# Eight visits of 128 tokens and one of 256 in the first list of a convolution and expert kernel, in place of ten of 128

## The chip, the core and the metric

The kernel runs on one core of one Trainium2 chip. A core has five engines that work side by side, each through its own queue in order: TensorE (PE, matmuls and transposes), VectorE (DVE), ScalarE (ACT), GpSimd (POOL) and SyncE (SP), which here only issues transfers. Sixteen DMA engines move data between the large memory (HBM) and the on-chip memory (SBUF). Results of matmuls lie in PSUM. The metric is the device time of one execution in microseconds.

## The reference, cut to what matters

```
w   = softmax(weight_gen) over 7 taps            # per token and head
x1  = sum over k of w[..., k] * x[token - 6 + k] # 8 heads of 24 columns, 8 x 2880 tokens
g   = argmax(x1 @ w_group)                       # 4 groups
e   = argmax(x1 @ w_expert[g])                   # 4 experts in each: 16 in all
out = p_g * p_e * (relu(x1 @ w1[g, e]) @ w2[g, e])   # 192 -> 1024 -> 192
```

All is fp32: 23,040 tokens of 192 columns, and every token goes through one of 16 experts, whose weights are 768 KB for each of the two matrices.

## The kernel before

**Groups.** The convolution runs over 15 groups of 12 tokens for each of the 128 partitions (1,536 tokens each), counted from 0. For a group SP loads the taps (`wt`, line 124) and the tokens (`xin`, line 134) into one of two buffers each; VectorE does the softmax and then 2 chunks of products (`pr`, line 317). The sums of the first chunks run on TensorE (line 358), later ones on VectorE (line 335). Then comes the routing: TensorE transposes and scores (lines 418 to 436), ScalarE copies between (lines 411 to 439), VectorE ranks, ScalarE's exponentials (line 375) and TensorE's counting matmuls (lines 476, 477) between, and GpSimd scatters the rows into `rows` in HBM, sorted by expert (line 531).

**Lists and visits.** After some groups `table` makes lists on VectorE (lines 553 to 621): which expert to visit, and from which row. ROUNDS says after how many groups, and how many visits of 384, 256 and 128 tokens. A visit loads one expert's weights and a block of its rows (`xb`, line 822). A visit of 128 in these rounds is plain: fp32 weights (`wa`, line 839, and `wc`, line 852), transposes at line 921. A visit of 256 loads the weights into `raw` (lines 841, 848) and splits them into a high and a low part (ScalarE lines 865 and 874, VectorE line 889); ScalarE copies part of the rows (`xd`, line 914), TensorE transposes them at line 932, and VectorE takes the low part of those too. Both then do the first matmul (line 958), a relu (line 967), the second matmul (line 1004), a scaling (line 1031) and a store of outputs (line 1042). A list of 128s is worked through in order of the experts. In the first list V1 to V10 are the visits of 128; the second list has four visits of 256, V11 to V14.

**What sets the order.** The program writes each engine's order down beforehand. `blocks` goes from unit to unit (a quarter of a visit here) and puts in what the next visits need; between the units `fill` takes steps of `front`, which yields the convolution and routing operation by operation, until a modelled VectorE clock has caught up. Loads of a visit are asked for three visits ahead (plain) or more. Two rules concern the change. In `front` (lines 716 and 717) the next group is loaded at one step of a group's convolution:

```
if n == (2 if state["slots"] else 0) and 1 <= g < ENDS[-1] - 1:
    load_group(g + 1)
```

and in `blocks` (lines 1128 to 1131) `slots` becomes true when the first visit that is not plain is opened:

```
if not b.plain:
    while state["open"]:
        assert step() is not False
    state["slots"] = True
```

SP issues its transfers in program order, and one that waits holds up all behind it.

Of the kernel before, what the change touches and what calls it, by code (L numbers as in the profile page):

```python
# [17 lines left out]
DRAM = bass.MemoryType.DRAM  # L18

WIDTHS = (12,) * 15  # L20
ROUNDS = ((2, 0, 0, 10), (3, 0, 4, 0), (4, 0, 5, 0), (5, 0, 7, 0), (6, 0, 5, 0), (7, 0, 7, 0), (8, 0, 5, 0), (9, 0, 6, 0), (10, 0, 7, 0), (11, 0, 5, 0), (12, 1, 4, 0), (13, 0, 5, 0), (14, 0, 6, 0), (15, 3, 2, 2))
SHORT = (7, 4)
LATE = (1.0, 3.0, 3.0)
AHEAD = (1.0, 1.0, 2.5)
# [18 lines left out]
def conv_moe_kernel(ctx: ExitStack, tc: tile.TileContext, x, wgen, w_group, w_expert, w1, w2, out):  # L43
# [26 lines left out]
    MAXB = NTOK // BK  # L70
    NR = len(ROUNDS)
    ENDS = [r[0] for r in ROUNDS]
    COL = [sum(WIDTHS[:g]) for g in range(len(WIDTHS) + 1)]
# [3 lines left out]
    TB = 3  # L77

    FIRST = ENDS[0]
    MAIN = next(r[0] for r in ROUNDS if r[1] or r[2])  # L80
    kinds = ((3, 1), (2, 2), (1, 3))
    CUT = {4: 3, 5: 2}
    rows_of = {1: UB, 2: 2 * UB, 3: 3 * UB, 4: 2 * UB + HB, 5: UB + HB}
# [2 lines left out]
    sure = 0  # L86
    for r in ROUNDS[:-1]:
        for nb, c in kinds:
            sure = max(sure, min(sure + nb * UB * r[c], COL[r[0]] * P - NE * (nb * UB - 1)))
    left = (NTOK - sure + NE * (BK - 1)) // BK  # L90
    TAIL = max(0, -(-(left - ROUNDS[-1][2]) // TB))

# [452 lines left out]
    def table(r):  # L545
# [14 lines left out]
        if last:  # L560
# [6 lines left out]
            for nb, odd, start, slots in ((4, half, at, SHORT[0]), (5, two, None, SHORT[1])):  # L567
# [4 lines left out]
                yield 0.6  # L572
        todo = [(nb, c) for nb, c in ((kinds[0], kinds[2], kinds[1]) if last else kinds) if ROUNDS[r][c] or last and nb == 2]
        for nb, c in todo:
# [97 lines left out]
    def front():  # L672
# [7 lines left out]
        def pace(g):  # L680
            return 99 if g <= FIRST else HURRY if g < MAIN + 3 else 8 if g in ENDS else 2

# [102 lines left out]

    order = []
    for r, spec in enumerate(ROUNDS):
        for nb, c in kinds:
            order += [(r, nb, q) for q in range(spec[c])]
            if r == NR - 1:  # L790
                order += [(r, k, q) for j, k in enumerate(CUT) if CUT[k] == nb for q in range(SHORT[j])]
# [479 lines left out]
```

## Time and profile before

| | |
|---|---|
| median of 3 runs | 1163.09 us (1161.98 to 1166.91) |
| the profiled execution | 1161.11 us, of which span 1159.1 us |
| TensorE busy | 1104.1 us (95%) |
| VectorE busy | 950.8 us (82%) |
| ScalarE busy | 648.5 us (56%) |
| GpSimd busy | 583.6 us (50%) |
| moved by DMA | 275.06 MB, mean 237 GB/s |

The span runs from the first to the last instruction. Busy shares are averages over stages with different limits, so the rows further down are taken by stage: the stage of the first list lies between 115 and 200 us. Durations of matmuls are pipelined; times between starts are the safer ones. PEclk is the granted TensorE clock, 1.00 for 2.4 GHz and 0.50 for 1.2 GHz. SPq stands for SP's issuing of transfers; their landing comes later.

### The profile page before, as it was taken

To read this page: it belongs to the slowest core of one execution; us is meant where nothing else is said; L and a number is where in the kernel's file an instruction comes from. 1 tells how busy PE (TensorE), PEld (TensorE's weight loads), DVE (VectorE), ACT (ScalarE), POOL (GpSimd) and SP (SyncE) were. 2 spreads that over 40 slices of the span, in tenths; PEclk is the share of its full clock that TensorE was granted. 3 is DMA by queue.
4 is the path that set the end of the run, shared out by engine and by line. 5 is a ranking of instruction groups with operands and counts; after the bars stand their busy time and mean duration, and the time that the engine had idled before them with its cause. 6 is when DMAs were issued, how large, how long until landed. Compare 5 with 4: busy or idle time off the path is not lost.

```text
span 1159.1 us, 23947 instructions
## 1 busy us (share of the span) xinstructions
PE 1104.1 (95%) x7941; PEld 1034.3 (89%) x7941; DVE 950.8 (82%) x1682; ACT 648.5 (56%) x1307; POOL 583.6 (50%) x613
## 2 busy tenths in 40 slices
PE   5786999999999999999999999999999999999997
PEld 2443888989999999999999999999999999999997
DVE  7899996989999998989898989998764676665661
ACT  1341344656556565665665656555646676667672
POOL 7064085738257573748374748475657321222211
PEclk9998998999999999999999999999999999999999
DMA  5698899986978787878797787876769886666562
GB/s 177 203 316 230 276 301 305 268 276 209 307 211 265 238 295 236 282 230 283 219 300 232 266 259 222 289 226 186 220 195 290 245 247 167 179 196 199 165 221 61
DMA packets 84342, 275.06 MB, mean 237 GB/s; under 512 B 15296, under 2 KB 34160, under 8 KB 82416
## 3 DMA queue, kind: packets, MB, share of 16 engines
q1 hardware_dynamic: 64056, 229.77, 64.1%
q0 software_dynamic: 20032, 43.39, 12.4%
q8 instruction: 64, 1.05, 0.4%
q14 instruction: 70, 0.57, 0.2%
q10 hardware_dynamic: 120, 0.28, 0.1%
HBM read 225.83 MB, written 47.88 MB: 236 GB/s over the span
## 4 chain that ended last, share of the span: by engine, by line
PE 74%; issue 8%; DVE 7%; DMA 4%; POOL 3%; ACT 2%; POOLq 1%; SPq 1%; DVEq 0%; ACTq 0%
PE ph L958 31%; PE py L1004 26%; PE py L1006 3%; DVE pr L317 3%; PE pl L401 2%; PE py L1007 2%; PE tpx L933 1%; PE tpx L932 1%; POOL out L1042 1%; PE ph L358 1%; DMA xb<-rows 1%; POOL rows L531 1%; DVE pr L353 1%; PE pl L1015 1%; PE tp L418 1%
## 5 line engine op out<-in xcount | busy, mean ns | idle before, releaser
L958 PE MATMUL ph<-xh,wa 128*128 128x256 f32 (+3 forms) x1992 | 453.4, 303 | 0.0
L1042 POOL DMA_INDIRECT out<-y,xb x189 | 214.8, 1136 | 402.7 <-ACT y L1031 168.7
L1004 PE MATMUL py<-wc,hh 128*128 128x192 f32 x2160 | 400.2, 326 | 0.0
L958 PE MATMUL ph<-xl,wa 128*128 128x256 f32 (+3 forms) x1328 | 350.0, 285 | 0.6 <-DVE xl L889 0.6
L1004 PEld LDWEIGHTS py<-wc,hh 128*128 128x128 f32 x2160 | 346.0, 190 | 0.0
L958 PEld LDWEIGHTS ph<-xh,wa 128*128 128x128 f32 x1992 | 335.5, 189 | 9.9 <-issue 8.4
L967 ACT ACTIVATE hh<-ph 128x512 f32<-128x512 f32 (+2 forms) x296 | 165.6, 559 | 258.5 <-PE ph L958 256.6
L317 DVE TENSOR_TENSOR pr<-xin,wt 128x1152 f32<-128x1152 f32 x186 | 249.3, 1351 | 5.6 <-PE py L358 3.5
L958 PEld LDWEIGHTS ph<-xl,wa 128*128 128x128 f32 x1328 | 250.8, 189 | 1.0 <-DVE xl L889 0.9
L531 POOL DMA_INDIRECT rows<-xrow,ix x156 | 223.5, 1433 | 46.9 <-POOL ix L530 35.6
L335 DVE TENSOR_TENSOR xrow<-xrow,pr 128x1152 f32<-128x1152 f32 x144 | 194.8, 1353 | 0.7
L889 DVE SCALAR_TENSOR_TENSOR pr<-ph,hh 128x256 fp32r<-128x256 f32 (+2 forms) x128 | 65.8, 514 | 79.7 <-ACT hh L972 42.3
L889 DVE TENSOR_TENSOR wa<-raw,wa 128x1024 fp32r<-128x1024 f32 x83 | 101.3, 1220 | 20.5 <-ACT wa L865 14.8
L530 POOL COPY ix<-posi 128x1 int32<-128x1 int32 x156 | 76.2, 500 | 61.7 <-DMA rows<-xrow,ix 31.9
L1006 PE MATMUL py<-wc,hh 128*128 128x384 f32 x320 | 101.2, 361 | 0.0
L972 ACT ACTIVATE hh<-ph 128x256 fp32r<-128x256 f32 (+2 forms) x128 | 59.0, 461 | 52.5 <-PE ph L958 52.5
L865 ACT CAST wa<-raw 128x1024 fp32r<-128x1024 f32 x83 | 87.2, 1050 | 0.0
L874 ACT CAST wa<-raw 128x1024 fp32r<-128x1024 f32 x83 | 86.4, 1041 | 0.0
L1007 PE MATMUL py<-wc,pr 128*128 128x192 f32 x320 | 80.1, 250 | 0.0
L1031 ACT ACTIVATE y<-py,xb 128x192 f32<-128x192 f32 x175 | 66.1, 425 | 22.0 <-PE py L1004 20.3
L889 DVE TENSOR_TENSOR xl<-tpx,xh 128x512 fp32r<-128x512 f32 (+1 forms) x83 | 56.5, 681 | 14.6 <-ACT xh L938 14.4
L1007 PEld LDWEIGHTS py<-wc,pr 128*128 128x128 f32 x320 | 60.9, 190 | 0.0
(205 smaller groups left out, 1325.6 us busy)
## 6 DMA issues: line engine op xcount, KB each, us to landing
wc<-in_moe_w SPq DMA_DIRECT2D x73, 768.0 KB
raw<-in_moe_w SPq DMA_DIRECT2D x83, 512.0 KB
xin<-in_x SPq DMA_DIRECT2D x14, 1728.0 KB
raw<-in_moe_w SPq DMA_DIRECT2D x91, 256.0 KB
raw<-w1lo SPq DMA_DIRECT2D x83, 256.0 KB
xb<-rows SPq DMA_DIRECT2D x75, 194.0 KB
wa<-in_moe_w SPq DMA_DIRECT2D x24, 384.0 KB
raw<-in_moe_w SPq DMA_DIRECT2D x11, 768.0 KB
```

The source lines that it names most:

```text
L317: nc.vector.tensor_tensor(out=dst, in0=o.xin[:, c0 + k:c0 + k + SC, :].rearrange("p s (h g) -> p s h g", g=HG), in1=w4[:, c0:c0 + SC, :, k ...
L335: nc.vector.tensor_tensor(out=acc, in0=acc, in1=prs[k - 2], op=ALU.add)
L531: written_once(nc.gpsimd.indirect_dma_start(out=rows[:, :], out_offset=bass.IndirectOffsetOnAxis(ap=ix, axis=0), in_=src, in_offset=None, ...
L865: nc.scalar.copy(out=o.wa[:, 0, :], in_=o.raw[0])
L874: nc.scalar.copy(out=o.wa[:, 2, :], in_=o.raw[1])
L889: f(*a, **k)
L958: nc.tensor.matmul(ph[:, v, :], lhsT=w[:, f0:f0 + P], rhs=rhs, start=i == 0, stop=i == len(terms) - 1)
L967: nc.scalar.activation(out=hh, in_=ph, func=AF.Relu)
L1004: nc.tensor.matmul(b.acc[t], lhsT=hh[:, v, c], rhs=wc[0][:, f, :], start=f == 0 and not (b.wide and t == 1), stop=f == NFT - 1 and not (b. ...
L1006: nc.tensor.matmul(b.py[t], lhsT=hh[:, v, c], rhs=wc[f // 4][:, f % 4].rearrange("p l d -> p (l d)"), start=f == 0, stop=False)
L1007: nc.tensor.matmul(b.acc[t], lhsT=hl[:, v, c], rhs=wc[f // 4][:, f % 4, 0, :], start=False, stop=f == NFT - 1)
L1042: ins = nc.gpsimd.indirect_dma_start(out=out[:, :], out_offset=bass.IndirectOffsetOnAxis(ap=b.x.bitcast(I32)[part, t, D + 1:D + 2], axis=0 ...
```

## The change

The first round's entry in ROUNDS becomes one visit of 256 and eight of 128; in the first round the 128s come first; MAIN keeps its value, 3. `table` makes the lists of a round from the larger visits to the smaller, so the first round now has two lists.

```
-ROUNDS = ((2, 0, 0, 10), (3, 0, 4, 0), ...
+ROUNDS = ((2, 0, 1, 8), (3, 0, 4, 0), ...
...
-    MAIN = next(r[0] for r in ROUNDS if r[1] or r[2])
+    MAIN = ENDS[1]
...
-        for nb, c in kinds:
+        for nb, c in kinds if r else kinds[::-1]:
             order += [(r, nb, q) for q in range(spec[c])]
```

V1 to V8 are now the visits of 128, V9 the visit of 256, and V10 is the first visit of the second list.

**SP, after the loads of V8 and V9.** Before: V9's last two rows stand first, then the taps and tokens of the sixth group (g = 5), then V11's raw weights.

```order
L852 ISA
L852 DMA wc_1650<-in_moe_w2 128x1536
L124 DMA wt_1662<-in_weight_gen 128x672
L134 DMA xin_1664<-in_x 128x3456
L836 TENSOR_LOAD tab2_1374
L836 ISA x2
L841 ISA
L841 DMA raw00_193<-in_moe_w1 128x1024
L848 ISA
L848 DMA raw10_195<-in_moe_w1 64x1024
L848 ISA
L848 DMA raw10_195<-w1lo_90 64x1024
```

Now, from the sixth group's taps and tokens on; ahead of them stands the first half of V11's raw weights, and the last row is V10's rows:

```order
L124 DMA wt_1722<-in_weight_gen 128x672
L134 DMA xin_1724<-in_x 128x3456
L848 ISA
L848 DMA raw10_195<-in_moe_w1 64x1024
L848 ISA
L848 DMA raw10_195<-w1lo_90 64x1024
L124 DMA wt_1794<-in_weight_gen 128x672
L134 DMA xin_1796<-in_x 128x3456
L820 TENSOR_LOAD tab2_1394
L820 ISA x2
L822 ISA
L822 DMA xb_175<-rows_89 128x388
```

The sixth group's loads stand there twice, within one visit's raw weights and ahead of V10's rows; the second pair waits for the transfers of the first. The convolution reads only the second pair. All other groups are loaded once.

**VectorE, at the first list** (`units` and `done` count an expert's tokens that are left and taken). Before, from the second operation of the table:

```order
L554 TENSOR_TENSOR units_794<-units_794,origin0_169 128x16
L558 SCALAR_TENSOR_TENSOR units_794<-units_794,done_163 128x16
L607 SCALAR_TENSOR_TENSOR cume_800<-smask12_158,units_794 128x16
L608 TENSOR_TENSOR cums_801<-cume_800,units_794 128x16
L609 TENSOR_SCALAR past_165<-cume_800,qp_151 128x16
```

Now, the first of 18 operations that stand between the second and the third of these:

```order
L558 SCALAR_TENSOR_TENSOR units_794<-units_794,done_163 128x16
L579 TENSOR_SCALAR n2_795<-units_794 128x16
L580 TENSOR_SCALAR n2_795<-n2_795 128x16
L607 SCALAR_TENSOR_TENSOR cume_802<-smask12_158,n2_795 128x16
L608 TENSOR_TENSOR cums_803<-cume_802,n2_795 128x16
L609 TENSOR_SCALAR past_165<-cume_802,qp_151 128x16
```

They make the list of the one visit of 256 and take its tokens off before the list of the 128s.

**ScalarE, around the routing of the third group** (`xT` and `ls` are the third group's transposed tokens and scores, `hh` the relus). Before, the copies of the routing follow one another:

```order
L424 COPY xT_1424<-tp_1673 128x384
L424 COPY xT_1424<-pl_1678 128x384
L431 COPY xT_1424<-pl_1683 128x384
L439 COPY ls_1697<-pl_1693 128x240
L967 ACTIVATE hh_1706<-ph0_1701 128x2x128
```

Now:

```order
L411 COPY rem_1726<-xrow_1027 128x384
L967 ACTIVATE hh_1737<-ph1_1732 128x2x128
L914 COPY xd1_180<-xb_175 128x256
L865 CAST wa_1742<-raw01_194 128x1024
L424 COPY xT_1470<-pl_1744 128x384
L424 COPY xT_1470<-tp_1749 128x384
L424 COPY xT_1470<-pl_1754 128x384
```

V9's copy of rows (line 914) and V10's cast (line 865) moved in front of the routing's copies.

## Rows read from the trace of the kernel before

**Rows 1.** The page's busy times: TensorE's share of the span.

```profile
PE 1104.1 (95%) x7941; PEld 1034.3 (89%) x7941; DVE 950.8 (82%) x1682; ACT 648.5 (56%) x1307; POOL 583.6 (50%) x613
```

**Rows 2.** Busy by stretch: us, PE, PEld, DVE, ACT, POOL, PEclk, DMA share, GB/s.

```profile
180.00:200.00 20.00, 17.31 (x113) 16.91 (x112) 12.37 (x39) 8.71 (x17) 9.53 (x11) 0.83 1.03 295
340.00:380.00 40.00, 40.00 (x305) 38.62 (x305) 36.37 (x43) 25.44 (x49) 30.44 (x26) 1.00 0.84 265
```

**Rows 3.** Timeline of TensorE: start, us, engine, line, operation, idle before and releaser.

```profile
110.78 0.91 PE L358 MATMUL tpx<-pr,ident 128*128 128x384 f32 x2 [1.73 <-DVE pr L353]
...
131.85 0.38 PE L921 MATMUL tp<-ident,xb 128*96 128x128 f32 x2
...
138.25 0.38 PE L921 MATMUL tp<-ident,xb 128*96 128x128 f32 x2
...
187.02 0.66 PE L921 MATMUL tp<-ident,xb 128*96 128x128 f32 x2 [2.69 <-DMA xb<-rows]
...
240.50 0.27 PE L932 MATMUL tpx<-ident,xb 128*128 128x128 f32 x1
...
329.13 0.27 PE L932 MATMUL tpx<-ident,xb 128*128 128x128 f32 x1
...
339.49 0.27 PE L932 MATMUL tpx<-ident,xb 128*128 128x128 f32 x1
```

**Rows 4.** Timeline of SP's issues in the first list's stage.

```profile
156.71 0.87 SPq L839 DMA_DIRECT2D wa<-in_moe_w  x2
...
176.74 0.35 SPq L822 DMA_DIRECT2D xb<-rows  x1
...
225.31 0.34 SPq L822 DMA_DIRECT2D xb<-rows  x1
```

**Rows 5.** Timeline of VectorE: the second round's list of 256s.

```profile
144.78 0.17 DVE L579 TENSOR_SCALAR n<-units 128x16 f32<-128x16 f32 x1
...
147.40 1.35 DVE L317 TENSOR_TENSOR pr<-xin,wt 128x1152 f32<-128x1152 f32 x1
```

**Rows 6.** DMA issues from 110 to 260 us: what, count, KB of one.

```profile
wc<-in_moe_w SPq DMA_DIRECT2D x16, 768.0 KB
wa<-in_moe_w SPq DMA_DIRECT2D x16, 384.0 KB
xin<-in_x SPq DMA_DIRECT2D x3, 1728.0 KB
raw<-in_moe_w SPq DMA_DIRECT2D x9, 512.0 KB
raw<-in_moe_w SPq DMA_DIRECT2D x9, 256.0 KB
xb<-rows SPq DMA_DIRECT2D x8, 194.0 KB
wt<-in_weight_gen SPq DMA_DIRECT2D x3, 336.0 KB
```

**Rows 7.** SP's DMA queue: packets, MB and share; 157 to 187, then 120 to 140 us.

```profile
q1 hardware_dynamic: 2100, 8.06, 83.5%
...
q1 hardware_dynamic: 1543, 6.12, 88.8%
```

**Rows 8.** Timeline of ScalarE at the first visit of 256.

```profile
195.42 0.40 ACT L914 COPY xd<-xb 128x256 f32<-128x256 f32 x1
195.72 1.05 ACT L865 CAST wa<-raw 128x1024 fp32r<-128x1024 f32 x1
```

**Rows 9.** Timeline of GpSimd: first and last scatter of two groups.

```profile
187.91 0.98 POOL L531 DMA_INDIRECT rows<-xrow,ix  x1 [0.33 <-POOL ix L530]
...
221.93 1.80 POOL L531 DMA_INDIRECT rows<-xrow,ix  x1 [0.28 <-DMA raw<-in_moe_w]
...
256.36 0.98 POOL L531 DMA_INDIRECT rows<-xrow,ix  x1 [0.16 <-POOL ix L530]
...
282.90 1.80 POOL L531 DMA_INDIRECT rows<-xrow,ix  x1 [0.28 <-POOL ix L530]
```

More of the change, by code (lines that the diff above doesn't have):

```diff
@@ L20 @@
 WIDTHS = (12,) * 15
-ROUNDS = ((2, 0, 0, 10), (3, 0, 4, 0), (4, 0, 5, 0), (5, 0, 7, 0), (6, 0, 5, 0), (7, 0, 7, 0), (8, 0, 5, 0), (9, 0, 6, 0), (10, 0, 7, 0), (11, 0, 5, 0), (12, 1, 4, 0), (13, 0, 5, 0), (14, 0, 6, 0), (15, 3, 2, 2))
+ROUNDS = ((2, 0, 1, 8), (3, 0, 4, 0), (4, 0, 5, 0), (5, 0, 7, 0), (6, 0, 5, 0), (7, 0, 7, 0), (8, 0, 5, 0), (9, 0, 6, 0), (10, 0, 7, 0), (11, 0, 5, 0), (12, 1, 4, 0), (13, 0, 5, 0), (14, 0, 6, 0), (15, 3, 2, 2))
 SHORT = (7, 4)
```

## Prediction

> **What bounds the kernel now.** I read the page first, then the busy times by stage, then TensorE's own timeline, and last the DMA answers, because TensorE turned out to stand still where a transfer was late. The page gives TensorE 95% of the span [rows 1]. By stages that splits in two: from 340 us on it is busy 40.00 of 40 us at full clock, so nothing there takes a delay back; between 180 and 200 us it is busy 17.31 of 20 and the granted clock is 0.83, which is time at 1.2 instead of 2.4 GHz [rows 2]. What is lost by then is lost at the end too. The timeline names the loss: the transposes of the tenth visit (V10; V1 to V10 are the visits of the first list before) start at 187.02 after 2.69 us of waiting for its rows, xb [rows 3]. SP issued that load at 176.74 [rows 4], so it lay some 10 us in the queue behind what had been issued ahead of it, the next group's x among them. That stretch is bound by the DMA queue, all else by TensorE, and ahead of 111 us by VectorE: the last products of the early convolution keep TensorE waiting 1.73 us at 110.78 [rows 3].
>
> **What the change does, part by part.** The reference's inputs put 167 to 262 tokens on each expert in the first two groups, and one expert has 256 or more. So V9, the new visit of 256, takes the two 128s that the same expert had before, and the other eight experts keep their visits: the coverage is equal, and later lists ask for the same rows. V10 is now the first visit of the second list.
>
> *Less work on TensorE.* Two plain visits of 6.40 us each (131.85 to 138.25) go, one of 10.36 us (329.13 to 339.49) comes [rows 3]: 12.80 - 10.36 = 2.4 us less. The split that V9 needs (two casts on ScalarE, two subtractions on VectorE) lies in front of it, beside plain visits.
>
> *A second list on VectorE.* In front of the list of 128s stands now the list of 256s, 18 small operations. The same list of the second round takes from 144.78 to 147.40 with 17 of them [rows 5]; one more makes 2.8 us. VectorE works without a pause up to the wait at 110.78, so this delays TensorE in full: +2.8. At least it is nothing (if the scatter of rows, which runs beside it, were what ends last), at most 2.8.
>
> *A group loaded twice.* This is what decides. The rule in `front` loads the next group at step 0 of a convolution while `slots` is false and at step 2 when it is true. `slots` turns true when the first visit that isn't plain is opened. That moves from V11 to V9, into the first steps of group 4, so both conditions hold once each: SP's order has wt and xin of the sixth group twice. The second pair goes to the same buffer and waits until the first has landed, with V10's rows right behind it on SP. In bytes [rows 6], from the loads of V8 on: before, V8 and V9 (768 + 97 + 768 each; xb of 128 tokens is half of the 194), wt + xin 2,064, raw of V11 1,024 (512 and twice 256, the second 256 out of w1lo), wa of V10 768, xb 97 = 7,219 KB ahead of and with V10's rows. Now: raw of V9 1,024, V8 1,633, raw of V10 1,024, xb and wc of V9 962, half of raw of V11 512, wt + xin 2,064, the other half 512, wt + xin again 2,064, xb 194 = 9,989 KB, that is 10.23 MB.
>
> When does that land? SP's first load of V8 is issued at 156.71 before [rows 4], now 2.8 later, and the queue is then never empty. SP's queue (q1) moved 8.06 MB in 157 to 187 us, 269 GB/s, and at its best 6.12 MB in 120 to 140 us, 306 GB/s [rows 7]. At 269: 10.23 / 0.269 = 38.0 us, landing at 159.5 + 38.0 = 197.5. At 306: 33.4 us, 192.9. The same sum for before gives 156.7 + 7.39 / 0.269 = 184.2, where TensorE got its rows at 187.0 [rows 3]: it is 2.8 early, since what is issued behind a load shares the engines with its last part. So the late end is 200.3. I take 197.5, from the row of the same stretch, between the two: early by that skew, late because the scatter of rows beside the queue is over in the last third.
>
> When is TensorE there? Before it was ready for V10's transposes at 187.02 - 2.69 = 184.33. Now: + 2.8 from the list; + 1.6 because ScalarE's copy of V9's rows and a 1.05 us cast (the two in [rows 8]) stand ahead of the copies that the third group's routing waits for, and V9's rows land only at 159.5 + 3,875 KB (3.97 MB) / 0.269 = 174.3; + 0.3 for what stands in front of this point in excess (two units of V9 in place of plain ones, less the routing sums that moved behind; the whole visit's saving above holds both). Ready at 189.1, so the wait is 197.5 - 189.1 = 8.4 us in place of 2.7, between 3.8 at the better rate and 11.2 at the late end.
>
> *The clock.* In 180 to 200 us it averages 0.83: 0.17 x 20 = 3.4 us lost, some 0.3 of it while TensorE stood still, so 3.1 [rows 2]. It fell after a wait of 2.7 us; a longer wait gives the same or a little less, since more of the slow time falls into the wait. I leave it at 3.1 (bounds 1.5 to 4).
>
> *The sum*: +2.8 (list) - 2.4 (work) + 1.6 (ScalarE) + 8.4 - 2.7 (the stall, new for old) + 3.1 - 3.1 (its clock) = +7.7. With the stall at 3.8 or 11.2, the clock between its bounds and the list at nothing it runs from -1 to +11. The profiled execution took 1161.1 us, so it would take 1168.8; it lies 2.0 under the median of the runs, 1163.1, so **1171 us** is forecast (1163.1 + 7.7, rounded).
>
> *What the page on DMA makes of it.* The rows show 295 GB/s of all queues in 180 to 200 us at a DMA share of 1.03 [rows 2], and SP's queue alone at 269 [rows 7]. The Trainium skill, "DMA: Bandwidth & Descriptors", section "Where 436 GB/s comes from", says that loads from HBM are limited to about 358 GB/s for a core, and under "Measured" that transfers of 1 MB reach 78% of the peak. By 358 the 10.23 MB would be an estimate of 28.6 us and V10's rows would land before TensorE asks; no run here shows that rate for SP's queue over such a stretch. It would make the third rival true.
>
> **Rivals.**
>
> *Late lists.* ScalarE's exponentials for the third group's ranking, and with them VectorE's ranking and list, stand now behind the copy of V10's rows, and TensorE's counting matmuls behind its transposes. They run at about 197.5 + 3.6 of work + 3.1 of slow clock = 204 instead of just ahead of 184, 20.5 later. The scatter that follows started at 187.91 and issued its last row at 221.93; the next group's took only 256.36 to 282.90; the next list's first load was issued at 225.31, 3.4 after the last row [rows 4, 9]. Now: 208.4 + 26.5 + 2.6 (two stores of outputs between) + 3.4 + 2 to land = 243. TensorE wants it at 240.50 + 7.7 = 248.2 [rows 3]. So there are 5 us to spare, and I count nothing. If the scatter takes 34.0 as before it lands at 250.5: 2.3 us of waiting and another 3.1 of clock, 1168.8 + 5.4 + 2.0 = 1176. For it: VectorE is over 90% busy up to 380 us [rows 2] and catches up little. Against it: the queue is emptier by then.
>
> *A small stall.* If the queue drains near 306 GB/s once the scatter beside it ends, the wait is 3.8, and with a milder clock (1.5) the sum is 7.7 - 4.6 - 1.6 = +1.5: 1164.6, no change that can be told.
>
> *No stall, and faster.* The place is the same, V10's rows; it decides at 10.23 MB in 189.1 - 159.5 = 29.6 us, 346 GB/s on SP's queue. Then the old stall goes with its clock and nothing replaces it: +2.8 - 2.4 - 2.7 - 3.1 + 0.8 (half of ScalarE's delay) = -4.6: 1158.5. For it: the queue did 306 once. Against it: both rows of q1, and the skew seen before.
>
> *The visit of 256 is empty.* If no expert had 256 tokens in the first list, V9 would work on padding and 256 tokens would come back as a further visit, +10.4 [rows 3]: 1181. The margin is 6 tokens of 262 and the inputs are fixed, so this is unlikely.
>
> **How the numbers follow.** The forecast has a chance of 0.50 (1167 to 1174), late lists 0.20 (1174 to 1182), the small stall 0.20 (1162 to 1166), no stall 0.07 (1157 to 1160), the empty visit 0.03. A measurement of this kernel can tell about 0.5%, 5.8 us, from no change, so slower means over 1168.9: three quarters of the forecast's share, all of the late lists and the empty visit, 0.61; faster means under 1157.3, which only the best of the no-stall case reaches, 0.05; the same 0.34. The range leaves out the no-stall case below and the ends above: 1160 to 1181.
>
> **What would show it.** In the profile after: a second xin of 1,728 KB within some 25 us of the first, with SP waiting for a DMA ahead of it; V10's first transposes (line 932) after a wait of 4 to 11 us for xb at about 190 to 200 us; a granted clock of 0.5 behind it; the first plain transposes (line 921) some 2.8 us later; eight plain visits of some 6.4 us and the ninth of some 10.4; no new wait of TensorE beyond 260 us. I am wrong if the wait at V10 is under 2 us (the queue is faster than I read it), if TensorE waits at the next lists' first visits (late lists), or if the first ten visits start no later (the list was hidden).

## The result, and the profile after

The changed kernel takes 1180.08 us (median of six runs, 1176.54 to 1182.17) against 1162.13 us for the kernel before on the same chip: a ratio of 1.0148, 95% interval 1.013 to 1.0166, that is 15 to 19 us slower. The profiled execution took 1182.17 us with a span of 1180.4; before it was 1159.1. The forecast of 1171 had the sign and the first stall right, and less than half of the loss. The measured time lies at the upper end of the stated range (1160 to 1181), which the prediction had kept for late lists, a rival with a chance of 0.20.

The page: busy times, which answer to [rows 1], and the loads of the groups' tokens (issues, KB of one, median us to landing).

```profile
PE 1107.4 (94%) x7917; PEld 1035.3 (88%) x7917; DVE 953.6 (81%) x1702; ACT 651.5 (55%) x1305; POOL 572.6 (49%) x613
...
xin<-in_x SPq DMA_DIRECT2D x15, 1728.0 KB, 12.8
```

TensorE is busy 3.3 us longer. The span grew by 21.3, so 18.0 us of it are standing still; and since the work on TensorE went down by 2.4 us (by the prediction's rows), some 5.7 us more of its busy time than before went to the slow clock. Where this is, the busy times by stretch show, with the columns of [rows 2]; the rows after the gap are wider stretches:

```profile
180.00:200.00 20.00, 14.28 (x104) 12.73 (x104) 8.52 (x23) 8.84 (x18) 3.98 (x5) 0.91 0.95 339
...
240.00:260.00 20.00, 16.88 (x115) 15.03 (x115) 14.48 (x25) 10.82 (x21) 4.54 (x5) 0.91 0.84 292
...
300.00:320.00 20.00, 17.57 (x120) 16.52 (x122) 18.68 (x17) 10.86 (x22) 6.77 (x8) 0.91 0.86 267
...
420.00:460.00 40.00, 30.60 (x215) 28.09 (x214) 34.50 (x35) 17.59 (x33) 26.26 (x23) 0.87 0.82 252
...
460.00:840.00 380.00, 380.00 (x2825) 370.25 (x2824) 350.03 (x617) 226.91 (x426) 218.41 (x218) 1.00 0.78 245
```

The forecast knew of one hole, at 180 to 200 us. There are three more beyond 240 us, the largest around 445 us, each with a granted clock under 1.00. From 460 to 840 us TensorE runs without a pause, so nothing is made good there. TensorE's timeline names the holes (columns and lines as in [rows 3]):

```profile
113.07 0.91 PE L358 MATMUL tpx<-pr,ident 128*128 128x384 f32 x2 [1.73 <-DVE pr L353]
...
134.90 0.38 PE L921 MATMUL tp<-ident,xb 128*96 128x128 f32 x2
...
141.30 0.39 PE L921 MATMUL tp<-ident,xb 128*96 128x128 f32 x2
...
170.38 0.42 PE L921 MATMUL tp<-ident,xb 128*96 128x128 f32 x2 [1.16 <-DMA xb<-rows]
...
179.47 0.44 PE L418 MATMUL pl<-ident,xrow 128*128 128x128 f32 x2 [2.72 <-ACT xT L424]
...
195.81 0.47 PE L932 MATMUL tpx<-ident,xb 128*128 128x128 f32 x1 [4.55 <-DMA xb<-rows]
...
229.63 0.27 PE L932 MATMUL tpx<-ident,xb 128*128 128x128 f32 x1
...
241.69 0.33 PE L932 MATMUL tpx<-ident,xb 128*128 128x128 f32 x1 [1.60 <-DMA xb<-rows]
...
247.88 0.38 PE L418 MATMUL pl<-ident,xrow 128*128 128x128 f32 x2
...
304.21 0.33 PE L932 MATMUL tpx<-ident,xb 128*128 128x128 f32 x1 [2.31 <-DMA xb<-rows]
...
449.82 0.47 PE L932 MATMUL tpx<-ident,xb 128*128 128x128 f32 x1 [9.40 <-DMA xb<-rows]
```

The row at 170.38 is V8, the last visit of 128, which already waits 1.16 us for its rows. The four waits for xb behind it stand at V10, V14, V19 and V31: each is the first visit of a list (the second, third, fourth and sixth). At V10 TensorE waits for the DMA queue, as forecast. At the other three it waits for something else, which SP's own waits show. First SP in 170 to 200 us, in the loads around V10; then SP in 225 to 245, in 285 to 306 and in 420 to 460 us, ahead of V14, V19 and V31; all as queue, line, what was waited for: us in total, times, longest:

```profile
SPq L134 <- DMA xin<-in_x: 5.9, 1, 5.9
SPq L124 <- DMA wt<-in_weight_gen: 5.2, 1, 5.2
...
SPq L822 <- DMA rows<-xrow,ix: 4.3, 1, 4.3
...
SPq L822 <- DMA rows<-xrow,ix: 4.9, 1, 4.9
...
SPq L822 <- DMA rows<-xrow,ix: 12.9, 1, 12.9
```

The first two are the sixth group's second loads of tokens and taps behind the first ones. The others are the loads of rows of V14, V19 and V31, which SP held back until GpSimd's scatter of those rows had landed. Such a wait of SP by itself costs nothing: ahead of the third and the fourth list it was 4.8 and 7.6 us in the kernel before, and TensorE did not wait there. What counts is whether the rows land before TensorE asks. Ahead of the sixth list SP's wait was shorter before (400 to 440 us):

```profile
SPq L822 <- DMA rows<-xrow,ix: 5.6, 1, 5.6
```

So the rows of V31 came late because they were sorted late. GpSimd's timeline, first and last scatter of the third list's group (g = 3, counted from 0; the one at 187.91 and 221.93 in [rows 9]; the prediction and the section on the change call it the third group) and of the sixth list's:

```profile
205.03 0.98 POOL L531 DMA_INDIRECT rows<-xrow,ix  x1 [0.33 <-POOL ix L530]
...
235.89 1.80 POOL L531 DMA_INDIRECT rows<-xrow,ix  x1 [0.28 <-POOL ix L530]
...
413.30 0.98 POOL L531 DMA_INDIRECT rows<-xrow,ix  x1 [0.16 <-POOL ix L530]
...
444.61 0.98 POOL L531 DMA_INDIRECT rows<-xrow,ix  x1 [0.28 <-POOL ix L530]
```

The same for the sixth list in the kernel before:

```profile
395.02 0.98 POOL L531 DMA_INDIRECT rows<-xrow,ix  x1 [0.15 <-POOL ix L530]
...
423.11 1.80 POOL L531 DMA_INDIRECT rows<-xrow,ix  x1 [0.28 <-POOL ix L530]
```

The third list's scatter starts 17.1 us later than before, the sixth's 18.3, and the first visit of the sixth list starts 19.4 later (449.82). In the kernel before it started after a wait of 0.39:

```profile
430.42 0.33 PE L932 MATMUL tpx<-ident,xb 128*128 128x128 f32 x1 [0.39 <-DMA xb<-rows]
```

Why the third list is late stands on VectorE's timeline:

```profile
185.22 0.69 DVE L889 TENSOR_TENSOR xl<-tpx,xh 128x512 fp32r<-128x512 f32 x1 [4.71 <-ACT xh L938]
...
197.32 0.20 DVE L480 TENSOR_REDUCE sme<-exe 128x12 f32<-128x48 f32 x1 [6.36 <-ACT exe L375]
```

and on ScalarE's:

```profile
177.69 0.41 ACT L914 COPY xd<-xb 128x256 f32<-128x256 f32 x1 [1.76 <-DMA xb<-rows]
...
195.79 0.41 ACT L914 COPY xd<-xb 128x256 f32<-128x256 f32 x1 [5.64 <-DMA xb<-rows]
...
197.05 0.24 ACT L375 ACTIVATE exe<-le 128x48 f32<-128x48 f32 x1
```

VectorE, which ranks the group, stands 4.71 us before V9's subtraction, because TensorE has only just transposed V9's rows (ScalarE, which had waited 1.76 us for these rows at 177.69, made the routing's copies late, and with them all that follows on TensorE), and 6.36 us before the sum of the exponentials, because ScalarE has them queued behind the copy of V10's rows. Some of VectorE's waits were there before as well, so the sum has to be taken against the kernel before. From the end of the first round's lists to the start of the third list's table (98.38 to 204.14 us; before 96.06 to 187.02) VectorE waits 15.2 us in place of 4.3, which is 10.9 more, and makes five subtractions of visits in place of one, 3.9 us more. With the 2.3 us by which the first list ends later (it costs 2.72 us, 93.42 to 96.14 on VectorE, which began it a little earlier) that is the 17.1.

### The profile page after: what moved, and what is told of

Read it like the earlier page. It is cut to its first block, busy times and chain, and to the rows that moved or that the text cites. A ratio compares the mean times of both kernels' runs of the same rounds, so it can differ in the third digit from the quotient of the medians.

```text
span 1180.4 us, 23897 instructions
## 1 busy us (share of the span) xinstructions
PE 1107.4 (94%) x7917; PEld 1035.3 (88%) x7917; DVE 953.6 (81%) x1702; ACT 651.5 (55%) x1305; POOL 572.6 (49%) x613
## 4 chain that ended last, share of the span: by engine, by line
PE 69%; issue 10%; DMA 6%; POOL 6%; DVE 6%; ACT 2%; SPq 0%; POOLq 0%; DVEq 0%; ACTq 0%
PE ph L958 29%; PE py L1004 24%; PE py L1006 3%; POOL rows L531 3%; DVE pr L317 2%; DMA raw<-in_moe_w 2%; POOL out L1042 2%; DMA xb<-rows 2%; PE pl L401 2%; PE py L1007 2%; PE tpx L933 1%; POOL ix L530 1%; PE tpx L932 1%; PE ph L358 1%; DMA rows<-xrow,ix 1%
## 5 line engine op out<-in xcount | busy, mean ns | idle before, releaser
L958 PE MATMUL ph<-xh,wa 128*128 128x256 f32 (+3 forms) x2016 | 460.7, 304 | 0.0
L1042 POOL DMA_INDIRECT out<-y,xb x189 | 211.0, 1117 | 426.5 <-ACT y L1031 189.0
L958 PE MATMUL ph<-xl,wa 128*128 128x256 f32 (+3 forms) x1344 | 354.8, 285 | 0.6 <-DVE xl L889 0.6
L958 PEld LDWEIGHTS ph<-xh,wa 128*128 128x128 f32 x2016 | 341.1, 190 | 10.0 <-issue 8.4
L958 PEld LDWEIGHTS ph<-xl,wa 128*128 128x128 f32 x1344 | 254.7, 189 | 1.0 <-DVE xl L889 0.9
L531 POOL DMA_INDIRECT rows<-xrow,ix x156 | 219.4, 1406 | 48.2 <-POOL ix L530 37.5
L530 POOL COPY ix<-posi 128x1 int32<-128x1 int32 x156 | 73.6, 483 | 66.7 <-DMA rows<-xrow,ix 33.9
```

The lines of the kernel that those rows point to most:

```text
L531: written_once(nc.gpsimd.indirect_dma_start(out=rows[:, :], out_offset=bass.IndirectOffsetOnAxis(ap=ix, axis=0), in_=src, in_offset=None, ...
L958: nc.tensor.matmul(ph[:, v, :], lhsT=w[:, f0:f0 + P], rhs=rhs, start=i == 0, stop=i == len(terms) - 1)
L1042: ins = nc.gpsimd.indirect_dma_start(out=out[:, :], out_offset=bass.IndirectOffsetOnAxis(ap=b.x.bitcast(I32)[part, t, D + 1:D + 2], axis=0 ...
```

## Experiments

Four theories were tried, two to begin with: (1) the second load, through V10's late rows, is the whole cause; (2) the extra list and the new order of ScalarE and VectorE cost on their own. Then (3): VectorE's busy time paces the lists, and TensorE's work ahead of 440 us is worth nothing; and (4): VectorE and TensorE wait for each other along the lists, and the end moves with the first visit of the sixth.

Each ratio is to runs of the kernel before on the same chip. Three chips took part, which differ a little: on that of the first four runs (one load or two, one list or two) the profiles have 2 to 9 us more behind some 440 us, as the table at the end of this section shows.

**One load in place of two.** The changed kernel with the guard, then with the later place only:

```
-if n == (2 if state["slots"] else 0) and 1 <= g < ENDS[-1] - 1:
+if n == (2 if state["slots"] else 0) and 1 <= g < ENDS[-1] - 1 and g + 1 not in grp:
...
+if n == (2 if state["slots"] or g == 4 else 0) and 1 <= g < ENDS[-1] - 1:
```

> The changed kernel with the sixth group (wt and xin) asked for once, at the earlier of the two places; order of TensorE, VectorE and ScalarE unchanged. Theory 1, the second load: V10's rows come 2,064 KB earlier on SP's queue (2.11 MB at 0.27 to 0.31 GB per ms, 7 to 8 us), at about 187, before TensorE asks at 191.3; so the 4.55 us wait at V10 goes, ScalarE's exponentials for the third group's ranking come some 8 us earlier (sme on VectorE at about 189 in place of 197.3), the scatter starts at about 196 in place of 205.0, and the waits at the first visits of later lists (1.6, 2.3 and 9.4 us) go or shrink below 1: 1162 to 1166 us. Theory 2, the order: ranking is late because it stands behind V10's copies at all; the wait at V10 and its clock go (6.3 us), but the later waits stay: 1172 to 1175 us.

> The changed kernel with the sixth group asked for once, at the later place, just ahead of V10's rows. The bytes ahead of V10's rows are the same as with the earlier load alone, so both theories give the same times as there, within 1 us: theory 1 (second load) 1162 to 1166 us, theory 2 (order) 1172 to 1175 us. If what costs is that SP waits at the second load for the landing of the first, and not its bytes, this run shows it too, since neither run has that wait.

Measured: 1.0112 (1.0083 to 1.0141) and 1.0102 (1.0076 to 1.0129). TensorE's timeline of the run with the later load only:

```profile
189.60 0.33 PE L932 MATMUL tpx<-ident,xb 128*128 128x128 f32 x1 [0.18 <-DMA xb<-rows]
...
237.14 0.47 PE L932 MATMUL tpx<-ident,xb 128*128 128x128 f32 x1 [4.18 <-DMA xb<-rows]
...
300.43 0.33 PE L932 MATMUL tpx<-ident,xb 128*128 128x128 f32 x1 [2.03 <-DMA xb<-rows]
...
445.97 0.48 PE L932 MATMUL tpx<-ident,xb 128*128 128x128 f32 x1 [8.83 <-DMA xb<-rows]
```

The wait at V10 is gone, and the third list's scatter starts at 197.8. But V14, which TensorE now reaches earlier, waits 4.18 in place of 1.60, and V31 still waits 8.83: it starts 3.9 us earlier, with some 6 us of wait and slow clock taken away at V10. Theory 1 as a cause of the whole falls. The second load is worth 2 to 4 us by the start of V31 in the two profiles, and 4 to 5 us by the ratios, which come from two chips. Theory 2's size fits better.

**The second load alone,** put into the kernel before:

```
+if (n == (2 if state["slots"] else 0) or g == 4 and n == 2) and 1 <= g < ENDS[-1] - 1:
```

> The kernel before (ten visits of 128, one list) with the sixth group asked for twice, the second time two steps of the convolution later. Theory 1 (second load): the rows of the first visits of the second list come 7 us later than before, at V10 (187.0) or at V11, with a wait of some 9 us in place of 2.7 and a later ranking of the third group only if it stands behind them: 1166 to 1178 us. Theory 2 (order): the wait alone, 6 us, and no more waits at later lists: 1166 to 1169 us.

Measured: 1.0039 (1.0021 to 1.0058), 4.6 us. V10 starts at 191.61 after 7.53 us of waiting (187.02 and 2.69 before), the rest of the queue behind it. From the other side this is the same size as above. Both expectations allow the time; V32 waits 1.50 us for its rows (0.39 before), which theory 2 did not expect.

**The second list alone:**

```
-if ROUNDS[r][c] or last and nb == 2]
+if ROUNDS[r][c] or r == 0 and nb == 2 or last and nb == 2]
```

> The kernel before with VectorE making a list of 256s in front of the first list of 128s, as the change does, but with no visit of it used: its 18 small operations alone. By the prediction's term the first visit's transposes (line 921) start 2.8 us later and the time rises by 2.8 us, to 1165; both theories agree if nothing else moves. Theory 2 (order) allows more, up to 1172 us, if a start 2.8 us later is enough to make later lists late; theory 1 does not.

Measured: 1.0044 (1.0019 to 1.0068), 5.1 us, where the forecast had 2.8. V1's transposes start 1.4 us later (116.22; 114.81 before), the third list's scatter 7.3 us later (195.16), and V20 and V32 wait 1.37 and 1.24 us for rows. The interval holds the 2.8 too, but the trace shows more than a later start: two lists come late that did not before (V20) or hardly (V32). Theory 1 doesn't allow for that. The edit also changed more than the 18 operations: the program, which paces the routing by its model of VectorE, now puts the routing's matmuls (line 418 on, 240.51) behind V15 (238.77), as the changed kernel does behind V14, where the kernel before has them in front (232.21, V15 at 240.50). So the 5.1 us are the list together with that order.

**The load moved behind V10's rows** in the kernel before, far and then a little less far (step 10 and step 8 of the convolution):

```
+if n == (10 if g == 4 else 2 if state["slots"] else 0) and 1 <= g < ENDS[-1] - 1:
```

> The kernel before with the sixth group's load (wt and xin) moved on SP's queue from ahead of V10's rows to some visits behind them; order of the other engines unchanged. The prediction's view (TensorE and the queue set the end): the 2.69 us wait at V10 and 3.1 us of slow clock behind it go and nothing takes their place, 5.8 us faster. New theory 3 (between 111 and 440 us VectorE sets the pace through the lists: each list comes when VectorE has ranked the group, and TensorE only has work in hand): V10 no longer waits, but the scatters start no earlier and the time is given back as a wait for the rows of V32 (0.39 us before), so within 2 us of before.

> The kernel before with the sixth group's load one step less far back than in the run that moved it behind: behind V10's rows and the weights of V12, but ahead of V11's rows. Order of the other engines unchanged. The prediction's view: V10's wait of 2.7 us and its 3.1 us of slow clock go, 5.8 us faster, ratio 0.995. Theory 4 (VectorE and TensorE wait for each other along the lists, and the end moves with the start of V32, the first visit of the sixth list, whose rows before come 0.39 us late): the end moves only as far as the sixth scatter (395.0 us before) does; the earlier V11 lets VectorE's subtractions of the visits go earlier, so 1 to 4 us faster, ratio 0.997 to 0.999.

Measured: 1.0017 (0.9997 to 1.0038) and 0.9999 (0.9986 to 1.0013). The 5.8 us of the prediction's view were not gained in either, nor the 1 to 4 us of theory 4 in the second. But neither is a clean test. In the first V10 waits no more, but the group itself comes late: VectorE waits 8.2 us for its taps, and TensorE for the ranking's copies:

```profile
205.73 0.47 PE L419 MATMUL tp<-ident,rem 128*128 128x128 f32 x1 [6.27 <-ACT rem L411]
```

In the second the wait has moved by one visit, to V11:

```profile
193.79 0.47 PE L932 MATMUL tpx<-ident,xb 128*128 128x128 f32 x1 [3.47 <-DMA xb<-rows]
```

What they do show is that the wait moves with the place of the load: V10's rows, V11's rows or the group's taps were waited for, 2.69, 3.47 and 8.2 us, according to which stood behind.

**Less work for TensorE** in the second list's visits of the kernel before (the slice keeps two products):

```
+...)[0:5 if b.o not in [visits[m] for m in range(10, 14) if m in visits] else 2]
```

> The kernel before with three of the five products of the first matrix left out in V11 to V14 (the four visits of the second list; their output lacks those terms): 24 matmuls of 0.117 us a visit, 11 us less work for TensorE between 196 and 240 us. The prediction's view: the end comes 11 us earlier, ratio 0.990. Theory 3: TensorE comes to the next lists' first visits earlier and waits there for rows that come when they did; with the slow clock behind the waits the ratio is 0.998 to 1.003.

Measured: 0.9961 (0.9942 to 0.998), 4.5 us of the 11, between the two views; theory 3's 0.998 is the end of the interval. The lists do come earlier with TensorE (the fourth's scatter at 250.04, before 256.36), but TensorE also waits for rows at V12, V20 and V32 (0.92, 1.03 and 1.52 us) and 2.3 us for VectorE, and over half is lost.

**More work for VectorE** in the kernel before:

```
+[product(c0, 0, acc) for _ in range(8 if g == 6 and n == 0 else 1)]
```

> The kernel before with one product of the seventh group's convolution on VectorE made eight times in place of once (7 x 1.35 = 9.5 us more on VectorE at about 335 to 350 us, the result the same, and no other engine has more to do). If TensorE sets the end and VectorE only runs beside it, nothing changes, within 2 us. Theory 4: the sixth list's scatter (395.0 us before) and the start of V32 come 8 to 10 us later and the end with them, plus up to 3 us of slow clock behind the wait: ratio 1.007 to 1.011.

Measured: 1.0048 (1.0026 to 1.007), 5.6 of 9.5 us, again some half. The products ran some 50 us earlier than I had put them, and it shows as a wait of TensorE for VectorE, with the clock at 0.91 in 300 to 320 us:

```profile
302.16 0.38 PE L958 MATMUL ph<-xl,wa 128*128 128x256 f32 x1 [2.89 <-DVE xl L889]
```

The sixth list's scatter came only 1.3 us later and V32 1.9 (432.27), so theory 4's path was wrong, though not that VectorE's time counts; where the rest of the 5.6 us lies, the profile of one execution does not show.

**VectorE's subtractions on GpSimd,** in the changed kernel with the later load only, and in the kernel before with the load moved far:

```
-..., nc.vector.tensor_tensor, ...
+..., (nc.gpsimd if n < 20 else nc.vector).tensor_tensor, ...
```

> The changed kernel with a single load of the sixth group (as in the run with the second load only, ratio 1.0102) and with the first subtraction of the weights' split (line 889, wa, 1.23 us each) on GpSimd in place of VectorE for V9 to V20: twelve of them, 14.8 us less on VectorE before the lists of V25 and later. Theory 3 (VectorE's pace): the waits of TensorE at the lists' first visits (4.2, 2.0, 0.5, 8.8 us) shrink by most of that and the ratio falls to 0.998 to 1.004. The order theory (ranking late because of what stands ahead of it on ScalarE) leaves it at 1.008 to 1.012.

> The kernel before with the sixth group's load behind V10's rows and the subtractions of V11 to V20 (ten, 12.3 us of VectorE) on GpSimd. Theory 3: the wait at V10 and its clock are now worth something, because the lists come earlier as well: ratio 0.994 to 0.997, and less than the load's move alone gives. The prediction's view: the same as the load's move alone, 0.995; so the two runs have to be read together.

Measured: 1.0427 (1.0398 to 1.0457) and 1.0146 (1.0117 to 1.0176). Theory 3, that VectorE's busy time alone is the pace, finds no support. In the first run the costliest groups of 110 to 480 us (columns as in the page's groups) hold, from GpSimd's and VectorE's lists:

```profile
L889 POOL TENSOR_TENSOR wa<-raw,wa 128x1024 fp32r<-128x1024 f32 x12 | 29.4, 2451 | 32.1 <-ACT wa L865 22.9 <-PE tpx L933 9.1
...
L889 DVE TENSOR_TENSOR xl<-tpx,xh 128x512 fp32r<-128x512 f32 x23 | 15.8, 689 | 32.7 <-ACT xh L938 32.4
```

GpSimd takes 2.45 us for what VectorE does in 1.22, stands 32 us waiting in its own order with the scatters behind it, and holds VectorE up while it works (last section), so this run didn't relieve VectorE as meant. What it shows is the second row: VectorE, with less to do, stands 32.4 us waiting for ScalarE's copies of rows that TensorE has just transposed (4.9 us in the run with the later load only). I read this as a loop: where TensorE waits for a list's rows (34.1 us in this run), VectorE waits with it, and the next list is late as well. The second run has mainly the fault of the load moved far: VectorE waited 18.1 us for the taps, and TensorE 15.16 behind it.

**V9 without VectorE,** in the changed kernel with the later load only:

```
+(o, "tw"), nothing if n == 8 else nc.vector.tensor_tensor, ...
+(b, "txl"), nothing if b.o is visits.get(8) else nc.vector.tensor_tensor, ...
```

> The changed kernel with a single load of the sixth group (ratio 1.0102), and V9 without its two subtractions on VectorE (1.23 us of its weights, 0.69 of its x; V9's five products are made with the upper halves alone, so its output lacks the small terms). Orders otherwise unchanged. If V9's place in VectorE's order is what the merge costs (VectorE, in order, waits there for ScalarE's copies, and the third list's ranking stands behind), the third list's scatter comes 3 to 5 us earlier than 197.8 and the end 2 to 5 us earlier: ratio 1.006 to 1.008. If the cost is that the first list holds less work for TensorE, the ratio stays at 1.009 to 1.011.

Measured: 1.0165 (1.0133 to 1.0197), above both. Nothing speaks for V9's two subtractions as what the merge costs: the third list's scatter starts at 200.1 without them and at 197.8 with them. Why a run with less work came out 0.6% above the one with 1.0102, on another chip, was not found; so differences of that size between runs on two chips should not be leaned on.

**Nine visits of 128 and the one of 256:**

```
-ROUNDS = ((2, 0, 1, 8), ...
+ROUNDS = ((2, 0, 1, 9), ...
```

> The changed kernel with a single load of the sixth group and nine visits of 128 in place of eight ahead of the 256 (ten visits in the first list): 6.4 us more work for TensorE ahead of the second list, and 128 tokens fewer for later. If the merge costs because the first list holds less work for TensorE, the waits at the next lists' first visits (4.2, 2.0, 0.5 and 8.8 us) shrink by about 6 us in all and the ratio is 1.003 to 1.007. If it costs by VectorE's and ScalarE's order, the lists come when they did, and the ratio is 1.009 to 1.013.

Measured: 1.0405 (1.0382 to 1.0429), outside both, for a reason of its own. The program ends with blocks of three visits, each of which runs only if tokens are left over, and one more of them ran: the matmuls of line 1006 (`py`, 384 columns) count 368 in place of 320, three visits of 16 more. From V32 to the end it takes 767.9 us in place of some 730. Ahead of that the run bears on the question. TensorE's waits from 230 to 460 us:

```profile
PE tpx L932 <- DMA xb<-rows: 0.6, 1, 0.6
```

and in the run with the later load only, which has eight:

```profile
PE tpx L932 <- DMA xb<-rows: 15.5, 4, 8.8
```

With one more visit in hand the waits at the lists are nearly gone, and the sixth list's scatter starts at 401.2 in place of 410.0, though VectorE has no less to do. The gain is smaller than the waits: the merged visit itself now waits 3.88 us for its rows (192.75), 6.4 us of work were added, and V32 starts 6.0 us earlier than V31 did (440.0; 446.0), still 9.6 later than before.

**All runs at one point.** Start of the first visit of the sixth list (V31 or V32, line 932), and from there to the end of the span, from each profile:

| run | sixth scatter starts | its first visit starts | from there to the end |
|---|---|---|---|
| before | 395.0 | 430.4 | 728.7 |
| after | 413.3 | 449.8 | 730.6 |
| earlier load only | 411.3 | 447.9 | 737.0 |
| later load only | 410.0 | 446.0 | 737.8 |
| before, two loads | 401.2 | 437.4 | 734.0 |
| before, two lists | 396.9 | 437.1 | 730.8 |
| before, load moved far | 395.4 | 430.3 | 727.1 |
| before, load moved less far | 395.2 | 430.8 | 729.9 |
| before, less work for TensorE | 389.9 | 426.4 | 728.8 |
| before, more work for VectorE | 396.3 | 432.3 | 730.9 |
| after, split on GpSimd | 438.2 | 474.2 | 732.0 |
| before, split on GpSimd and load moved far | 415.1 | 450.0 | 731.6 |
| after, V9 off VectorE | 412.6 | 448.6 | 730.0 |
| after, nine of 128 | 401.2 | 440.0 | 767.9 |

The first visit moves by 48 us over these runs, the rest, but for the last run, by 11, and by 5 without three runs on the chip of the first four (737.0, 737.8, 734.0). So most of a run's difference is made by the time TensorE starts the sixth list. In the runs that wait there it is the list's rows that decide; in three (load moved far, split on GpSimd and load moved far, nine of 128) TensorE comes to them without a wait, and it is what stood in its way before. No run with all of its work beats the kernel before.

## Why the prediction was right or wrong

**The list, +2.8: right.** 2.72 us on VectorE, and V4 starts 3.05 us later (141.30; 138.25 in [rows 3]). With the order that comes with it, it costs 5.1 us (2.2 to 7.9) alone; lateness of the lists is not in the term.

**The group loaded twice: right in kind.** There are 15 loads of xin, the second of the sixth group waiting 5.9 us on SP and its wt 5.2 us before that, with V10's rows behind them. The sum by bytes took SP's queue as never empty; these 11.1 us of waiting are not in it.

**ScalarE, +1.6 and 0.3: too small.** TensorE was ready for V10 at 195.81 - 4.55 = 191.3, the forecast had 189.1. The routing's transposes waited 2.72 us for ScalarE, which itself waited for V9's rows (there at 177.7, forecast 174.3), and V8 waited 1.16 us for its own rows, a stall that the forecast did not have.

**The stall at V10, 8.4 in place of 2.7: over-sized by 3.85.** The rows came at 195.8 (forecast 197.5), and TensorE 2.2 us later than forecast. SP's queue carried 10.42 MB in 160 to 196 us, 289 GB/s, between the 269 that the forecast took and the 306 of its other bound [rows 7]; the rival without a stall needed 346. The Trainium skill, "DMA: Bandwidth & Descriptors", section "Where 436 GB/s comes from", speaks of about 358 GB/s, which this queue didn't come near. All queues together moved 339 GB/s in 180 to 200 us and passed that figure for short (439 in 180 to 182 us).

**The clock, +3.1 and -3.1: over-sized at V10.** It reads 0.91 in 180 to 200 us, 1.8 lost. So by V13, which starts at 229.63 where V14 before started at 225.54, the loss is 4.1 us and not the 7.7 of the sum.

**"No new wait beyond 260 us": the step that failed.** The late-lists rival, at 0.20, came true, and larger than its price. The forecast worked the third list's rows out well: scatter at 208.4 (205.0), last row 234.9 (235.9), landing 243 (241.7). What failed is "TensorE wants it at 240.50 + 7.7 = 248.2": it was there at 241.69 - 1.60 = 240.1. Half of the error is the 7.7 that was 4.1. The other half is order, which TensorE's timeline before shows:

```profile
225.54 0.28 PE L932 MATMUL tpx<-ident,xb 128*128 128x128 f32 x1
...
232.21 0.38 PE L418 MATMUL pl<-ident,xrow 128*128 128x128 f32 x2
...
236.48 0.55 PE L436 MATMUL pl<-ident,xT 128*128 128x128 f32 x3 [0.60 <-ACT xT L431]
```

Before, these matmuls of the routing stand ahead of that list's first visit and take some 4.6 of the 14.96 us between 225.54 and 240.50; now they stand behind it, at 247.88. The 5 us of spare were not there. And the forecast stopped at this one list: it didn't look at V19 and V31, where 2.31 and 9.40 us were waited with slow clocks around them. Of the 21.3 us in the profile 4.1 are there by V13, 15.3 more by V31, and 1.9 come after. That the measured time still lies in the range is owed to the rival, not to the forecast's own sum.

**"Bound by the DMA queue, all else by TensorE": half wrong.** The prediction read TensorE's 40.00 of 40 us in 340 to 380 as proof for all that follows [rows 2]; and its "VectorE is over 90% busy up to 380 us" holds for that stretch, not for 180 to 200 us, where the same rows have 12.37 of 20. Up to 430 us the kernel before sits on an edge, with a wait of 0.39 us at V32. On that edge 11 us less of TensorE's work gave 4.5, and 9.5 us more of VectorE's cost 5.6.

**What the runs attribute:** of the 17.2 us that 1.48% is, the second load alone is 4.6 (2.5 to 6.8) and the second list alone 5.1 (2.2 to 7.9). The rest, some 7.5 if the parts simply add and carry over from the chip that they ran on, goes with the merged visit; the run without V9's subtractions gives no sign that it is V9's work on VectorE. That the first list holds less work for TensorE fits the run with nine visits, where the waits went. The scatters say the same. Against the kernel before, those of the third, fourth, fifth and sixth lists start later by 9.9, 9.5, 12.6 and 15.0 us with the later load only (nine visits in the first list), but by 7.3, 7.1, 0.7 and 1.9 us with the second list alone and by 14.6, 12.7, 5.1 and 6.2 us with nine visits of 128 and the one of 256 (ten visits each). Those with ten make most of it good behind the fourth list, the one with nine does not. These are single profiles, and how much of the 7.5 is this and how much the order of ScalarE's copies was not separated and stays open. The 2.4 us of work were saved where TensorE then waited.

## What to carry to other kernels

Where one engine makes the lists another works from, read the margin at every hand-over, not only at the next one: for each list, when its rows land and when the consumer asks. A consumer at 100% on both sides of a hand-over that it waits 0.39 us for, as at the sixth list here, has no margin there; saving its work ahead of that point is in part paid back as a wait (4.5 of 11 us were gained), and a delay of the producer is in part passed on (5.6 of 9.5 us). A flag that other code reads (here `slots`) makes moving the place where it is set a change of that code too.

## What the runs showed of the hardware that was not expected

**GpSimd holds VectorE up.** In the first run with the split on GpSimd, GpSimd's timeline has these two subtractions of 128x1024 in SBUF:

```profile
195.71 2.36 POOL L889 TENSOR_TENSOR wa<-raw,wa 128x1024 fp32r<-128x1024 f32 x1 [9.06 <-PE tpx L933]
...
282.24 2.40 POOL L889 TENSOR_TENSOR wa<-raw,wa 128x1024 fp32r<-128x1024 f32 x1
```

and VectorE's, at the same times:

```profile
196.04 2.06 DVE L482 SCALAR_TENSOR_TENSOR smg<-sme,smg 128x12 f32<-128x12 f32 x1
...
281.58 4.28 DVE L317 TENSOR_TENSOR pr<-xin,wt 128x1152 f32<-128x1152 f32 x1
```

The small operation takes 0.17 us in the changed kernel (at 197.56) and the product 1.35: they took 1.9 and 2.9 us longer, about what GpSimd's work lasts. An operation with one input (line 480, at 195.80) took its usual 0.20 us inside that work. So a subtraction moved to GpSimd saved VectorE 1.22 us and cost it 1.9 and 2.9 in these two places, where the two met. The Trainium skill, "GPSIMD Engine Reference", section "Specifications", says that GpSimd shares its way into SBUF with VectorE, with contention for VectorE's operations with two inputs in SBUF; these rows agree. The Trainium skill, "Perfetto Trace Analysis", section "Optimizing Scalar/DVE Operations", says that offloading even to GpSimd may make sense where VectorE is saturated, and warns that it might not help since the two share a port; here the warning held.

**The slow clock was not longer behind a longer wait.** Around V10's 4.55 us in the changed kernel the granted clock is 0.90 in 194 to 196 us, where TensorE still stood, and then under 1.00 in two more slices of 2 us (columns as in [rows 2]):

```profile
196.00:198.00 2.00, 2.00 (x9) 1.75 (x8) 0.65 (x3) 2.00 (x5) 0.00 (x0) 0.50 1.02 419
198.00:200.00 2.00, 2.00 (x14) 2.00 (x13) 2.00 (x2) 1.60 (x3) 0.84 (x1) 0.75 1.04 271
```

Behind the 2.69 us of the kernel before it is, from 186 to 194 us, 0.59, 0.50, 0.50 and 0.70. Around V31's 9.40 us it reads 0.69 in 444 to 446, 0.50 from 446 to 454 and 0.75 in the next slice, half of that while TensorE stood still. And around the routing's 2.72 us in the changed kernel, which end at 179.47, it stayed at 1.00.
